# A second Strassen level in the first layer of a fused retention and MLP kernel

## The chip, the cores and the metric

The kernel runs on one core of a Trainium2 chip. The metric is the device time of one execution in microseconds (us), the median of the runs. A profile is one execution; its span runs from the first to the last instruction and is a little shorter than the device time.

Names used below: **TensorE** (PE in the profile) does matrix products, with PEld for the loading of its stationary operand; **VectorE** (DVE) and **ScalarE** (ACT) do elementwise work; GpSimd is POOL, and SyncE (SP) starts most of the DMAs. PSUM is the memory that TensorE writes into[...].

## The reference, cut to what matters

```python
def _attn_ref(q, k, v):                      # (4, 8, 768, 64) each: batch, heads, seq, head_dim
    gamma = 1.0 - 2.0 ** (-5.0 - np.arange(H, dtype=np.float32))
    for t in range(S):                       # retention: a state that decays, per head
        state = gamma * state + k[t] (outer) v[t]
        y[t] = scale * q[t] @ state

def _moe_ref(x, w_in, w_out):                # x (3072, 512), w_in (512, 2048), w_out (2048, 512)
    h = x @ w_in
    g = np.maximum(0.01 * h, h)              # leaky ReLU
    return (g @ w_out).astype(np.float32)
# reference: y becomes x, (batch*seq, heads*head_dim); the weights come in as float64
```

The two big products are the two layers, `x @ w_in` and `g @ w_out`. All of it is computed in fp32.

## The kernel before

The sequence is cut into six chunks of 128 time steps (times 4 batches: 512 tokens), and the 2048 hidden features into four units of 512. For each chunk `c` and unit `u` there is a first-layer step `hidden(c, u)` and a second-layer step `output`. Both are a 2x2 block product done by Strassen's scheme (in Winograd's form): seven products M1 to M7 of 256 x 256 x 256 blocks in place of eight, with sums of blocks made beforehand (`differences`, `add_sums`) and sums of products made afterwards (`takes`).

```python
def seven(tiles, name, takes, takes_piece=None, order=ORDER):
    banks = {}
    which = [("M1", "A", 0, 0), ("M6", "B", 5, 5), ("M5", "C", 4, 4), ("M4", "D", 3, 6),
             ("M2", "A", 2, 2), ("M7", "B", 1, 1), ("M3", "C", 6, 3)]
    for m, bank, sa, sb in (which[i] for i in order):
        ...                                       # a bank is [128, 2, 256] fp32: one PSUM bank
            for to, (i, a, z) in places:          # i = 0, 1: halves of the 256 output features
                for n, (w, x, t) in enumerate(tiles):
                    for k in range(2):
                        nc.tensor.matmul(to, lhsT=block(w, sa)[:, k, ts(i, 128)],
                                         rhs=rhs[:, k, a:z], start=..., stop=...)   # L585
            takes(m, ps)
        yield

def hidden(c, u, x, t, g, gd, order=ORDER):
    def leaky(i):
        nc.scalar.activation(g[:, i], g[:, i], AF.Prelu, alpha=0.01)                # L620
    def takes(m, ps):
        if m == "M1":
            nc.scalar.copy(out=got["m1"], in_=ps)                                   # L625
        elif m == "M6":
            plus(got["u2"], got["m1"], ps)                                          # L527
        elif m == "M5":
            nc.scalar.copy(out=got["m5"], in_=ps)
        elif m == "M4":
            got["m4"] = ps
        elif m == "M2":
            nc.scalar.activation(g[:, 0], ps, AF.Prelu, alpha=0.01)
        elif m == "M7":
            u3 = got["m1"]
            plus(u3, u3, ps)
            plus(g[:, 3], u3, got["m5"]);  leaky(3)
            plus(g[:, 2], u3, got["m4"]);  leaky(2)
        elif m == "M3":
            plus(g[:, 1], got["u2"], ps);  leaky(1)
            differences(g, gd)                                                      # L530
```

`output` has the same form, with nine VectorE additions where it adds to an earlier unit's result. Chunks 0 and 1 run together, unit by unit, while VectorE and ScalarE turn the float64 weights into fp32 (`round_piece`). From chunk 2 on, two units are done one after the other and their second layers are accumulated together in PSUM:

```python
for c in range(2, NC):
    for p in range(NU // 2):
        pair = []
        for u in (2 * p, 2 * p + 1):
            pair.append(new_g(c, u))
            run(hidden(c, u, *xs[c], *pair[-1][1:]), {})
        ...
        run(output(c, os[c], pair, p == 0, last), at)
        ...                        # visit_with_scores: the retention of the next chunk
```

## Time and profile before

| | before |
|---|---|
| device time, median of 2 runs | 657.12 us (656.94 to 657.3) |
| span of the profile | 655.4 us |
| PE busy | 650.6 us, 99% |
| DVE busy | 361.5 us, 55% |
| ACT busy | 176.1 us, 27% |
| DMA | 49.00 MB, mean 75 GB/s |
| DVE busy from 60 to 205 us (chunks 0 and 1) | 125.3 of 145 us |
| DVE busy from 344 us to the end | 124.3 of 311.4 us |

A row of the timeline gives the start of a run of like instructions, its length, the engine, the line, the operation, what it writes and reads, the tile's shape and how many there are; "[2.65 <-DVE g L527]" is the idle time of the engine before it and what ended it. An fp32 matmul appears as two records of TensorE, so "x8" is four matmuls. Records overlap[...]: the pace is read from the starts, not from the lengths.

### The profile page before, as it was taken

The page shows a single profiled execution, that of the slowest core. Times are in us where ns is not written, and L with a number is a line of the kernel's source. Part 1 is how long each engine was busy: PE and PEld are TensorE (multiplying, and loading weights), DVE is VectorE, ACT ScalarE, POOL GpSimd, SP SyncE. Part 2 cuts the span into 40 slices and gives each one's busy share as a digit, 9 for nine tenths or more (in the row PEclk, how much of TensorE's full clock was granted, in tenths as well). Part 3 has the DMA queues.
Part 4 walks back from the last instruction along what each step waited for, and adds up shares of the span by engine and source line. Part 5 has one row for each costly group of instructions (what it writes and reads, how often), then busy time and mean ns, then how long its engine had stood idle before and what let it go on. Part 6 is the DMA issues. An engine that isn't in the chain of part 4 may idle for free.

```text
span 655.4 us, 11361 instructions
## 1 busy us (share of the span) xinstructions
PE 650.6 (99%) x4937; PEld 568.2 (87%) x4937; DVE 361.5 (55%) x590; ACT 176.1 (27%) x323; POOL 22.7 (3%) x45
## 2 busy tenths in 40 slices
PE   8999999999999999999999999999999999999998
PEld 5888888888888888888888889888888888888887
DVE  5789969889887664243436414527423344431342
ACT  5855464264261003102102211300220210221210
POOL 1000000000000020000001001001000100000000
DMA  9921312323322650030022003005001001000001
GB/s 337 406 98 37 125 64 97 97 66 111 115 78 82 243 179 0 1 129 2 1 103 91 1 1 130 1 17 179 0 1 61 5 1 49 17 0 1 1 0 65
DMA packets 15906, 49.00 MB, mean 75 GB/s; under 512 B 1768, under 2 KB 2152, under 8 KB 15856
## 3 DMA queue, kind: packets, MB, share of 16 engines
q1 hardware_dynamic: 15696, 47.72, 20.7%
q8 instruction: 39, 0.64, 0.4%
q10 hardware_dynamic: 160, 0.55, 0.2%
q14 instruction: 11, 0.09, 0.0%
HBM read 41.97 MB, written 6.29 MB: 74 GB/s over the span
## 4 chain that ended last, share of the span: by engine, by line
PE 98%; DMA 1%; DVE 0%; ACT 0%; SPq 0%; issue 0%
PE B_o L585 13%; PE A_o L585 13%; PE C_o L585 13%; PE A_h L585 12%; PE B_h L585 12%; PE C_h L585 12%; PE D_o L585 6%; PE D_h L585 6%; PE ap L182 2%; PE d L607 2%; PE yp L255 2%; PE yp L219 1%; DMA raw<-in_weights_dram 1%; PE yp L244 1%; PE sp L270 1%; PE yp L270 0%
## 5 line engine op out<-in xcount | busy, mean ns | idle before, releaser
L585 PE MATMUL A_h<-x,w 128*128 128x256 f32 x368 | 87.7, 381 | 0.0
L585 PEld LDWEIGHTS A_h<-x,w 128*128 128x128 f32 x368 | 69.3, 190 | 9.6
L585 PE MATMUL A_o<-g,w 128*128 128x256 f32 x288 | 68.1, 379 | 0.0
L527 DVE TENSOR_TENSOR m<-m,B_h 128x512 f32<-128x512 f32 x23 | 15.8, 686 | 93.3 <-PE B_h L585 93.3
L585 PEld LDWEIGHTS A_o<-g,w 128*128 128x128 f32 x288 | 54.6, 190 | 7.5
L620 ACT ACTIVATE g<-g 128x512 f32<-128x512 f32 x69 | 42.0, 630 | 66.3 <-DVE g L527 66.3
L625 ACT COPY m<-A_h 128x512 f32<-128x512 f32 x23 | 13.5, 585 | 169.3 <-PE A_h L585 149.0
L527 DVE TENSOR_TENSOR m<-m,B_o 128x512 f32<-128x512 f32 x16 | 11.0, 685 | 64.4 <-PE B_o L585 64.4
L585 PE MATMUL B_h<-t,w 128*128 128x256 f32 x184 | 43.7, 380 | 0.0
L585 PE MATMUL C_h<-x,w 128*128 128x256 f32 x184 | 43.5, 379 | 0.0
L585 PE MATMUL C_h<-t,w 128*128 128x256 f32 x184 | 43.5, 379 | 0.0
L585 PE MATMUL D_h<-t,w 128*128 128x256 f32 x184 | 43.5, 379 | 0.0
L585 PE MATMUL B_h<-x,w 128*128 128x256 f32 x184 | 43.5, 379 | 0.0
L585 PEld LDWEIGHTS B_h<-t,w 128*128 128x128 f32 x184 | 34.7, 190 | 5.2 <-DVE t L530 0.6
L585 PEld LDWEIGHTS C_h<-x,w 128*128 128x128 f32 x184 | 35.0, 190 | 4.8
L585 PEld LDWEIGHTS D_h<-t,w 128*128 128x128 f32 x184 | 35.0, 190 | 4.8
L585 PEld LDWEIGHTS C_h<-t,w 128*128 128x128 f32 x184 | 35.0, 190 | 4.8
L585 PEld LDWEIGHTS B_h<-x,w 128*128 128x128 f32 x184 | 35.0, 190 | 4.8
L585 PE MATMUL C_o<-gd,w 128*128 128x256 f32 (+1 forms) x148 | 34.2, 373 | 0.0
L585 PE MATMUL C_o<-g,w 128*128 128x256 f32 (+1 forms) x148 | 34.2, 373 | 0.0
L530 DVE TENSOR_TENSOR gd<-g,gd 128x512 f32<-128x512 f32 x48 | 33.2, 692 | 1.7
L585 PE MATMUL B_o<-gd,w 128*128 128x256 f32 x144 | 34.1, 380 | 0.0
(131 smaller groups left out, 984.6 us busy)
## 6 DMA issues: line engine op xcount, KB each, us to landing
raw<-in_weights_dram SPq DMA_DIRECT2D x31, 512.0 KB, 3.9
kv<-in_kv_dram SPq DMA_DIRECT2D x17, 512.0 KB, 5.0
out_dram<-o SPq DMA_DIRECT2D x23, 256.0 KB, 2.1
qk<-in_qk_dram SPq DMA_DIRECT2D x10, 512.0 KB, 4.6
o<-in_qk_dram SPq DMA_DIRECT2D x8, 512.0 KB, 4.9
in<-in_qk_dram SPq DMA_DIRECT2D x5, 512.0 KB, 8.4
in<-in_kv_dram SPq DMA_DIRECT2D x3, 512.0 KB, 7.9
kv<-in_kv_dram SPq DMA_DIRECT2D x4, 256.0 KB, 7.4
```

Source lines behind the costliest of these rows:

```text
L182: nc.tensor.matmul(to, lhsT=x[ts(j, 64), 1, a, ts(late, 64)], rhs=x[ts(j, 64), 0, a, late * 64 :])
L219: mm = nc.tensor.matmul(ps[ts(i, 64), j, m, :], lhsT=st[b][ts(j, 64), a, :], rhs=x[ts(j, 64), 0, a, :], start=(m == 0), stop=False, skip_g ...
L244: mm = nc.tensor.matmul(ps[ts(i, 64), j, m, 0:64], lhsT=y[ts(s, 64), 1, 2 * a + j, :], rhs=am[ts(s, 64), j, m, 0], start=False, stop=True, ...
L255: nc.tensor.matmul(ps[ts(i, 64), j, m, 64:], lhsT=y[:, 1, 2 * a + j, :], rhs=am[:, j, m, 1 + (i ^ j)], start=(c == 0 and m == 0), stop=Tru ...
L270: nc.tensor.matmul(sp[ts(j, 64), a, :], lhsT=y[:, 0, 2 * a + j, :], rhs=y[:, 1, 2 * a + j, :], start=start, stop=True, skip_group_check=True)
L527: nc.vector.tensor_tensor(out=out, in0=a, in1=b, op=ALU.add)
L530: nc.vector.tensor_tensor(out=out, in0=a, in1=b, op=ALU.subtract)
L585: nc.tensor.matmul(to, lhsT=block(w, sa)[:, k, ts(i, 128)], rhs=rhs[:, k, a:z], start=(first and (i == 0 or split) and n == 0 and k == 0), ...
L607: nc.tensor.matmul(banks[r][:, i, :], lhsT=block(2 * u, r + 2 * kh)[:, k, ts(i, 128)], rhs=x[:, 2 * kh + th, k, :], start=(step == 0 and i ...
L620: nc.scalar.activation(g[:, i], g[:, i], AF.Prelu, alpha=0.01)
L625: nc.scalar.copy(out=got["m1"], in_=ps)
```

## The change

The first layer of chunks 2 to 5 gets a second Strassen level. Each of the seven 256 x 256 x 256 products M1 to M7 becomes seven products of 128 x 128 x 128: 49 matmuls of 128 moving columns in place of 28 of 256 columns. The aim is fewer columns on TensorE. The sums of weights that the inner level needs are made once by VectorE while chunks 0 and 1 run, stored in DRAM (`kept`), and loaded again for each chunk and unit. The outer products are done in two groups, of four and of three, so that one inner product for all of a group fits one PSUM bank.

A second idea runs through the whole kernel: instead of VectorE adding M1 and M6, ScalarE copies M1 into the PSUM bank in which M6 is then accumulated. TensorE then adds M6 (and M7) to it. [...]a small bf16 matmul (`fill`) goes through it. The order of the seven products changes with this.

```diff
+    kept = [dram.tile([128, 7, 7, C], FP32, name=f"kept_{u}") for u in range(NU)]
+        def do():                          # sum_of_unit: 4 of these for each of 4 units
+            if i == 0:   plus(s[0], a21, a22)          # each [128, 7, 128]
+            elif i == 1: minus(s[1], s[0], a11)
 ...
-    ORDER = (0, 1, 2, 3, 4, 5, 6)
+    ORDER = (0, 2, 1, 3, 4, 6, 5)
+    FUSED = (0, 2, 1, 4, 5, 6, 3)          # M1, M5, M6, M2, M7, M3, M4
+    LAST = (0, 2, 1, 3, 4, 5, 6)
 ...  hidden, now for chunks 0 and 1 alone
             if m == "M1":
-                got["m1"] = temp("m1", at)
-                nc.scalar.copy(out=got["m1"], in_=ps)
+                nc.scalar.copy(out=to, in_=ps)         # to = bank_of("B")
             elif m == "M6":
-                plus(got["u2"], got["m1"], ps)
+                nc.scalar.copy(out=got["u2"], in_=ps)
 ...  output
+            elif m == "M7":
+                if fused:
+                    nc.scalar.copy(out=bank_of("D"), in_=ps)   # M4 accumulates on it
+                add(3, ps)
 ...  the first layer of chunks 2 to 5
+    INNER = (("M1", 0, 0, 0), ("M5", 1, 3, 2), ("M4", 2, 2, 4), ("M6", 3, 4, 3), ("M2", 0, 1, 1),
+             ("M3", 1, 5, 5), ("M7", 3, 6, 6))
+    def inner(n, group):
+        w, count = ((wa, 4), (wb, 3))[group]
+        for m, q, j, s in INNER:
+            for i in range(count):
+                nc.tensor.matmul(ps[q][:, i], lhsT=w[:, j, i], rhs=part_of(moving[i], s),
+                                 start=(i == 0 and m in ("M1", "M5", "M4")), stop=True, ...)
+            if m == "M1":   nc.scalar.copy(out=ps[3], in_=ps[0])
+            elif m == "M5": nc.scalar.copy(out=sums[:, 3], in_=ps[1])
+            elif m == "M4": nc.scalar.copy(out=sums[:, 2], in_=ps[2])
+            elif m == "M6": nc.scalar.copy(out=sums[:, 1], in_=ps[3])
+            elif m == "M2": nc.scalar.copy(out=sums[:, 0], in_=ps[0])
+            elif m == "M3": plus(sums[:, 1], sums[:, 1], ps[1])
+            elif m == "M7":
+                plus(sums[:, 3], sums[:, 3], ps[3])
+                plus(sums[:, 2], sums[:, 2], ps[3])
+        load_unit(n + 1, group)             # the next unit's weights, by DMA
+
+    def outer(n, group):
+        if group == 0:
+            plus(u2, u2, m1)
+            plus(to(1), u2, m5)
+            return
+        plus(to(0), m1, m2);    leaky(0)    # leaky: ScalarE, to(i): a block of g
+        plus(to(1), to(1), m3); leaky(1)
+        plus(u2, u2, m7)
+        plus(to(3), u2, m5);    leaky(3)
+        plus(to(2), u2, m4);    leaky(2)
 ...
+    for n in range(N2):                     # 16: chunk 2 + n // 4, unit n % 4
+        if n + 1 < N2:
+            differences(*gs[n][1:])
+            inner(n + 1, 0)
+            outer(n + 1, 0)
+        if visiting:                        # retention of the next chunk, at units 0 and 1
+            joint_visit(...)
+        steps = output(c, os[c], [gs.pop(n)], ..., order=FUSED if more else LAST)
+        products(steps, 4)                  # M1, M5, M6, M2
+        if visiting:
+            fill(3)
+        ...
+        if more:
+            inner(n + 1, 1)
+            outer(n + 1, 1)
+        products(steps, 3)                  # M7, M3, M4
```

The second layers of two units are no longer accumulated together; each unit has an `output` of its own. The retention of the chunks 3 to 5 (`joint_visit`) uses the same matmuls as before in banks 4 to 7.

## The prediction

> **What bounds the kernel now.** I read the page's busy line first, then the chain of work that ended last, then the timeline of a quiet stretch, and last the windows by stage.

> ```profile
> PE 650.6 (99%) x4937; PEld 568.2 (87%) x4937; DVE 361.5 (55%) x590; ACT 176.1 (27%) x323; POOL 22.7 (3%) x45
> PE 98%; DMA 1%; DVE 0%; ACT 0%; SPq 0%; issue 0%
> ```

> TensorE is busy throughout and is 98% of the chain: any column taken off it is time saved, and any wait put on it is time lost. Its busy time alone could hide gaps, so I look at starts. From 406 to 414 us of the timeline, first-layer products and what follows them:

> ```profile
> 406.11 1.89 PE L585 MATMUL B_h<-x,w 128*128 128x256 f32 x8
> 407.83 1.89 PE L585 MATMUL C_h<-x,w 128*128 128x256 f32 x8
> 408.03 0.69 DVE L527 TENSOR_TENSOR m<-m,B_h 128x512 f32<-128x512 f32 x1 [6.15 <-PE B_h L585]
> 408.82 0.69 DVE L527 TENSOR_TENSOR g<-m,m 128x512 f32<-128x512 f32 x1
> 409.43 0.68 DVE L527 TENSOR_TENSOR g<-m,D_h 128x512 f32<-128x512 f32 x1
> 409.55 1.83 ACT L620 ACTIVATE g<-g 128x512 f32<-128x512 f32 x3 [2.65 <-DVE g L527]
> 409.56 1.89 PE L585 MATMUL A_h<-x,w 128*128 128x256 f32 x8
> 411.49 0.58 ACT L625 COPY m<-A_h 128x512 f32<-128x512 f32 x1
> ```

> Four matmuls start every 1.727 us, without a gap. A step of seven is 12.09 us. The reader should also see the chain after M7: VectorE starts 0.20 us after TensorE has gone on; a following addition starts 0.79 us later if it needs the last result and 0.61 us later if not; ScalarE's leaky ReLU starts 0.04 us after its input; the copy behind the three leaky ReLUs starts only when they end.

> The kernel has a few matmuls of 128 columns already, at its very end:

> ```profile
> 645.48 1.03 PE L585 MATMUL B_o<-g,w 128*128 128x256 f32 x4
> 646.34 1.03 PE L585 MATMUL B_o<-g,last 128*128 128x256 f32 x4
> ...
> 651.10 0.61 PE L585 MATMUL C_o<-g,last_s 128*128 128x128 f32 x4
> 651.55 0.61 PE L585 MATMUL C_o<-g,w 128*128 128x128 f32 x4
> 652.00 0.61 PE L585 MATMUL C_o<-g,last_s 128*128 128x128 f32 x4
> ```

> Two matmuls of 256 columns start every 0.865 us, two of 128 every 0.45 us: 0.432 and 0.225 us each.

> [...]half the columns cost 52% of the time (0.225 of 0.432 us), although each record here loads new weights.[...] No copy into PSUM is in the trace before.[...] The reloaded weights come in runs of 512, 1024 and 1536 B. The trace before has mostly runs of 3 KB and tells nothing of these.

> **The change, part by part.**

> TensorE, first layer of chunks 2 to 5: 28 x 0.432 = 12.10 us becomes 49 x 0.225 = 11.03 us. Sixteen times 1.07 is **-17.1 us**. The second layer keeps its columns, and so does retention.

> VectorE: an addition of 512 elements is 0.69 us, one of 384 is 0.553 us (the masking row of that shape). Per unit, the inner level has 3 x 0.69 + 3 x 0.553 = 3.7 us, the outer sums 7 x 0.69 = 4.8, the differences of g 4 x 0.69 = 2.8, the second layer 6 x 0.69 = 4.1: 15.4 us, with retention and the sums of x about 79 us a chunk, beside 11.03 + 12.10 us of TensorE a unit and 5 us for each of two visits, 102 us a chunk. So VectorE goes from 40% in this stretch (124.3 of 311.4 us) to over 75%, but isn't the bound on average. The question is its latency where TensorE needs it.

> I go through the order of one iteration of the new loop, with E the moment when TensorE has issued the last matmul of inner group 1. On TensorE follow M7, M3 and M4 of the second layer, 1.73 us each. M4 accumulates on bank D, into which ScalarE must first copy M7. In ScalarE's queue this copy stands behind the four leaky ReLUs of the unit just made, and they wait for VectorE's outer sums:

> - E + 0.20: VectorE adds the inner M7 to two sums of 384 elements, the second 0.47 us later (0.61 us, less 128 elements at about 1 ns, which is the slope between the two shapes).
> - the block g0 needs that: E + 1.25. Then g1 and u2 at 0.61 us each, g3 after u2 (0.72 to 0.79 us), g2 0.61 us later: it starts at E + 3.8 and ends at E + 4.5.
> - its leaky ReLU: E + 4.5 to E + 5.15. The copy of M7, 0.585 us: E + 5.7. With a hop to TensorE: **E + 5.8**.
> - TensorE without a wait would start M4 at E + 3.45.

> So TensorE waits **2.35 us** before M4, in each of the 15 iterations that have a next unit. Nothing gives it back, since TensorE is the bound. **+35 us.**

> Other waits I looked at and take as nothing: M6 of the second layer waits for the copy of M1, but M5's 1.73 us lie between; the inner M6 waits for the copy of the inner M1, with 1.35 us (M5 and M4 of the three) against about 0.8; the differences of g end at about E + 11, the next second layer begins at E + 13.8.

> Entering the new loop: the first inner group follows the first unit's leaky ReLUs closely, and its M6 waits for a copy in the same queue: +1.5 us. Thirteen fill matmuls, some 0.25 us each: +3 us. In the last visits no scores hide the taking of tokens: +0.7 us.

> Chunks 0 and 1: VectorE is 86% busy there (125.3 of 145 us). Each step of seven loses two additions (some 15 steps, -20 us of VectorE), the weight sums add sixteen of 896 elements, 1.08 us each by the same slope (+17 us). It stays as full as before, and where three tasks meet, around unit 3's retention, TensorE may wait a little: +3 us, a guess.

> DMA: a unit's weights are 49 blocks of 64 KB, 3.2 MB, in about 25.5 us: 126 GB/s, below the 406 GB/s that a slice of the page shows. The larger group (1.84 MB) has some 19 us from its release to its use. I take it as hidden.

> Sum: 657.1 - 17.1 + 35 + 1.5 + 3 + 0.7 + 3 = 683; I say **682 us**.

> **The rivals.**

> - *The copy does not hold M4 up*, because the chain is shorter than I built it. Then about 648 us remain, 1.4% faster. For it: the intent of the change, and an average load of VectorE of 75%. Against: the queue order, which I take as fixed, and seven additions in a row of which none is under 0.47 us.
> - *The 128-column matmuls run slower in the mass*[...]. Then there is no gain in columns: with 0.25 us instead of 0.225, 16 x 49 x 0.025 = 20 us more, so near 700. For it: only sixteen records of that shape are in the trace. Against: those are evenly spaced.
> - *The reload of weights comes late*[...]: the inner groups would start with a wait on DMA, at 100 GB/s about as long as the window. Then over 690 us. Against: the windows of nearly 20 us and few other transfers.
> - *VectorE becomes the bound in chunks 0 and 1*: at most the 14% free there turns negative; I'd expect up to 10 us.

> **Range and chances.** The wait can be 1.5 to 3 us (22 to 45 us in all), the rest 2 to 12 us against the sure -17: 665 to 695 us. To be slower by over 2% (above 670.3) the wait has to be over some 1.5 us; to be faster by over 2% (below 644) all of my extra terms would have to vanish and more. Hence 0.04 faster, 0.22 same, 0.74 slower.

> **What would show it.** In the profile after, the inner matmuls should start every 0.225 us, or 6.3 and 4.7 us a group. The waits should have TensorE waiting for the M7 copy, about 2.3 us, 15 times, seen as a gap before the product into bank 6, with four leaky ReLUs and then a copy into bank 6 on ScalarE just ahead. VectorE should be near 75% busy there. I am wrong if that gap is under 1 us, if gaps before the inner groups end on DMA, or if the first part (up to the start of the new loop, 237 us before) has moved by more than 8 us.

## The result, and the profile after

The changed kernel takes **718.38 us** (718.01 to 718.76, two runs): 1.0933 times the kernel before [1.0901, 1.0965]. It is 61.3 us slower, where the prediction had 682 us and a range up to 695. The direction and the main wait were foreseen; the size was not.

The page of the kernel after: the busy line, the clock granted to TensorE in 40 slices, and the chain that ended last.

```profile
PE 665.6 (93%) x5583; PEld 590.7 (82%) x5583; DVE 473.0 (66%) x782; ACT 265.1 (37%) x495; POOL 23.2 (3%) x45
...
PEclk9999999999999899999999999999999999999998
...
PE 78%; DVE 14%; ACT 4%; DMA 2%; issue 2%; DVEq 0%
```

TensorE was 99% busy and is 93% busy, and VectorE and ScalarE have entered the chain with 14% and 4%. There is a puzzle in the first line. The second level takes columns off TensorE, yet its busy time *rose* by 15 us, from 650.6 to 665.6. The clock line hides the reason: nearly every slice shows 9, which is "90% or more". The mean over the whole span is 0.963, against 1.000 before. A mean of 0.963 can be 3.7% everywhere or one half for a few us at a time.

The waits of TensorE in the kernel after (what waited and for what: us in total, times, longest):

```profile
PE bank L536 <- ACT bank L646: 32.0, 15, 2.1
PE bank L569 <- DVE o L480: 6.3, 1, 6.3
PE bank L156 <- issue: 3.2, 2, 2.7
...
PE bank L1036 <- DMA wa<-kept: 0.9, 1, 0.9
```

L646 is the copy of M7 into bank D, L536 the second-layer products (M4 here), L1036 the inner products, L569 a fill matmul, L156 the retention's scores. The predicted wait is there, 15 times. The timeline shows what follows it. One iteration on TensorE, starts and lengths in us:

```profile
556.15 3.62 PE L536 MATMUL bank<-g,w 128*128 128x256 f32 x16
561.91 3.66 PE L536 MATMUL bank<-gd,w 128*128 128x256 f32 x8 [2.13 <-ACT bank L646]
565.40 0.39 PE L1036 MATMUL bank<-x,wa 128*128 128x128 f32 x2
...
578.57 4.85 PE L1036 MATMUL bank<-x,wb 128*128 128x128 f32 x42
583.25 3.62 PE L536 MATMUL bank<-g,w 128*128 128x256 f32 x16
589.01 3.62 PE L536 MATMUL bank<-gd,w 128*128 128x256 f32 x8 [2.13 <-ACT bank L646]
```

The first row is M7 and M3, sixteen records in 3.62 us. The row after it is M4, eight records of the same shape in 3.66 us: half the pace. From M4's start to the next product is 3.49 us where M4 took 1.73. In windows of 1 us around that wait (window, its length, PE busy and number of records, granted clock, DMA share, GB/s):

```profile
560.00:561.00 1.00, 0.00 (x0) 1.00 1.12 349
561.00:562.00 1.00, 0.09 (x1) 0.95 1.18 285
562.00:563.00 1.00, 1.00 (x3) 0.50 0.16 37
563.00:564.00 1.00, 1.00 (x4) 0.50 0.00 0
...
565.00:566.00 1.00, 1.00 (x8) 0.84 0.00 0
566.00:567.00 1.00, 1.00 (x12) 1.00 0.00 0
```

The clock is one half right behind the wait, for about 3.4 us, and then whole again. TensorE counts as busy all the while, which is why its busy time rose. The prediction has no such term.

To count these, I took windows of 8.2 us, from the moment TensorE stops, around each of the 15 waits. In twelve the mean clock is about 0.79. In three (waits that end at 382.93, 502.37 and 532.61 us) it stays at 1.00. One of each kind, same columns:

```profile
353.65:361.85 8.20, 6.07 (x32) 0.79 0.34 101
380.73:388.93 8.20, 6.07 (x47) 1.00 0.60 191
```

The wait is equally long in both; 32 records pass in one and 47 in the other. So a wait costs 2.13 us, and in twelve cases 8.2 x 0.21 = 1.72 us more. That is 20.6 us in all, over half as much again as the waits themselves.

On ScalarE the wait ends as the prediction drew it:

```profile
585.30 1.23 ACT L1070 ACTIVATE g<-g 128x512 f32<-128x512 f32 x2 [2.71 <-DVE g L480]
587.24 1.23 ACT L1070 ACTIVATE g<-g 128x512 f32<-128x512 f32 x2 [0.70 <-DVE g L480]
588.37 0.58 ACT L646 COPY bank<-bank 128x512 f32<-128x512 f32 x1
```

Four leaky ReLUs (L1070), each released by VectorE, then the copy, and M4 at 589.01.

**An account of the +61.3 us**, from the trace after:

| | us | from |
|---|---|---|
| fewer columns, 16 units | -18 | 12.09 - 10.95 each |
| M4 waits for the copy, 15 times | +32.0 | waits |
| halved clock after twelve of these | +20.6 | 1.72 each |
| the first part, up to the end of the new loop's first unit (both inner groups) | +13 | 261.1 us, against 237.0 + 10.95 |
| standstills in the visits (2.74, 0.44, 0.75) and the clock after one | +5.6 | "issue" in the waits and timeline |
| fills in the visits | +2 | ten of 0.16 to 0.22 |
| one wait on reloaded weights | +0.9 | waits |
| not assigned | +5 | remainder |

The first part is measured up to the same work in both traces: in the one before to the first product of chunk 2 (first row), in the one after to the first product of its second unit (second row), which lies one first-layer unit, 10.95 us, further on:

```profile
237.01 1.99 PE L585 MATMUL A_h<-x,w 128*128 128x256 f32 x8
...
261.08 0.38 PE L1036 MATMUL bank<-x,wa 128*128 128x128 f32 x2
```

Of its 13 us, 6.3 are one wait and some 1.9 the halved clock behind it. The timeline at that place:

```profile
230.95 1.15 DVE L483 TENSOR_TENSOR x<-t,x 128x384 f32<-128x384 f32 x2
...
232.48 1.28 DVE L480 TENSOR_TENSOR o<-o,B_o 128x512 f32<-128x512 f32 x2
...
233.82 1.03 PE L569 MATMUL bank<-mask 128*128 128x512 bf16 x2 [6.34 <-DVE o L480]
```

Here TensorE's banks pass from the old loop to the new one. The additions of the last old step (`o<-o,B_o`) stand in VectorE's queue behind the sums of chunk 2's x, and the first fill of the new loop waits for them.

### The profile page after: what moved, and what is told of

It reads as the page before. It is cut to its first block, busy times and chain, and to the rows that moved or that the text cites. A ratio compares the mean times of both kernels' runs of the same rounds, so it can differ in the third digit from the quotient of the medians.

```text
span 717.0 us, 13274 instructions
## 1 busy us (share of the span) xinstructions
PE 665.6 (93%) x5583; PEld 590.7 (82%) x5583; DVE 473.0 (66%) x782; ACT 265.1 (37%) x495; POOL 23.2 (3%) x45
## 4 chain that ended last, share of the span: by engine, by line
PE 78%; DVE 14%; ACT 4%; DMA 2%; issue 2%; DVEq 0%
PE bank L1036 25%; PE bank L536 24%; DVE g L480 4%; DVE made L480 3%; PE A_o L536 3%; PE C_h L536 3%; PE B_h L536 3%; ACT g L1070 3%; PE B_o L536 2%; PE A_h L536 2%; PE C_o L536 2%; PE d L557 2%; PE D_o L536 2%; PE D_h L536 1%; DMA wa<-kept 1%
## 5 line engine op out<-in xcount | busy, mean ns | idle before, releaser
L480 DVE TENSOR_TENSOR o<-o,bank 128x512 f32<-128x512 f32 (+2 forms) x91 | 58.7, 662 | 83.6 <-PE bank L536 65.3
L536 PE MATMUL bank<-gd,w 128*128 128x256 f32 x288 | 79.2, 431 | 26.3 <-ACT bank L646 25.6
L536 PEld LDWEIGHTS bank<-gd,w 128*128 128x128 f32 x288 | 59.7, 211 | 40.6 <-ACT bank L646 30.4
L536 PE MATMUL bank<-g,w 128*128 128x256 f32 x384 | 91.0, 386 | 0.3 <-DVE x L269 0.3
L536 PEld LDWEIGHTS bank<-g,w 128*128 128x128 f32 x384 | 72.2, 193 | 10.2 <-DVE x L269 0.5
L1036 PEld LDWEIGHTS bank<-x,wb 128*128 128x128 f32 x672 | 77.6, 192 | 1.4
L1036 PE MATMUL bank<-x,wb 128*128 128x128 f32 x672 | 77.6, 275 | 0.0
L1036 PE MATMUL bank<-x,wa 128*128 128x128 f32 x512 | 71.0, 282 | 0.0
L1036 PEld LDWEIGHTS bank<-x,wa 128*128 128x128 f32 x512 | 67.8, 201 | 2.5 <-ACT bank L1040 0.2
L1070 ACT ACTIVATE g<-g 128x512 f32<-128x512 f32 x64 | 39.4, 630 | 54.6 <-DVE g L480 54.6
L1036 PE MATMUL bank<-t,wa 128*128 128x128 f32 x384 | 57.4, 289 | 0.9 <-DMA wa<-kept 0.9
L1036 PEld LDWEIGHTS bank<-t,wa 128*128 128x128 f32 x384 | 52.5, 207 | 1.1 <-DMA wa<-kept 1.1
L536 PE MATMUL bank<-gd,last 128*128 128x256 f32 (+1 forms) x124 | 29.1, 389 | 6.4 <-ACT bank L646 6.4
L536 PEld LDWEIGHTS bank<-gd,last 128*128 128x128 f32 x124 | 23.4, 197 | 10.8 <-ACT bank L646 7.6
L536 PE MATMUL bank<-g,last 128*128 128x256 f32 x120 | 30.5, 403 | 0.0
L536 PEld LDWEIGHTS bank<-g,last 128*128 128x128 f32 x120 | 24.2, 206 | 3.9 <-issue 0.3
L536 PE MATMUL A_h<-x,w 128*128 128x256 f32 x112 | 26.6, 380 | 0.0
```

The lines of the kernel that those rows point to most:

```text
L480: nc.vector.tensor_tensor(out=out, in0=a, in1=b, op=ALU.add)
L536: nc.tensor.matmul(to, lhsT=block(w, sa)[:, k, ts(i, 128)], rhs=rhs[:, k, a:z], start=(first and (i == 0 or split) and n == 0 and k == 0), ...
L1036: nc.tensor.matmul(ps[q][:, i], lhsT=w[:, j, i], rhs=part_of(moving[i], s), start=(i == 0 and m in ("M1", "M5", "M4")), stop=True, skip_gr ...
```

## The experiments

Each kernel is timed against the kernel before on the same chip (657.4 to 657.5 us there). The first four start from the kernel after.

**The copy of M7 ahead of the leaky ReLUs.** M7 is computed right after the inner group, so its copy enters ScalarE's queue before the four leaky ReLUs.

```diff
             inner(n + 1, 1)
+            products(steps, 1)
             outer(n + 1, 1)
...
-        products(steps, 3)
+        products(steps, 2 if more else 3)
```

> Theory A: in the changed kernel TensorE waits 2.13 us before M4 in 15 iterations because the copy of M7 into M4's bank stands behind four leaky ReLUs in ScalarE's queue, and in 12 of these a halved TensorE clock follows for about 3.4 us and costs 1.7 us more. Here the second layer's M7, its copy and its addition are issued ahead of the outer sums; the work is the same. A expects no gap before M4, no halved clock in the loop, 15 x 2.13 + 12 x 1.72 = 52.6 us less than 718.4, so 666 us. Rival B, that the clock falls because the matmuls are short and dense and not because of the gap: only the 32 us of waiting go, 686 us, and the clock stays at about 0.96. Rival C, that the wait comes back elsewhere because VectorE's outer sums now begin later: a new wait on VectorE before the next second layer, 675 us or more.

Measured: 666.81 us, ratio 1.0142 [1.011, 1.0174], mean clock 0.992. No wait on the copy is left. Fifty-two us come from the order of one copy in a queue; that is 32.0 + 20.6 to within about 1 us. So the place in the queue holds M4, not the copy's own time, and the clock's loss hangs on that wait.

**Filler: is it the idle time that halves the clock?** Here the wait stays, but TensorE works through it: ten (or five) bf16 fill matmuls into a bank that is free.

```diff
-        products(steps, 3)
+        products(steps, 2)
+        for _ in range(10 if more else 0):     # 5 in the second kernel
+            fill(0)
+        products(steps, 1)
```

> The changed kernel with ten bf16 matmuls of 512 columns, about 2.15 us in all, put into the gap before M4, into a bank that nobody reads. They do not remove the wait, they only keep TensorE at work during it. Theory A (an idle stretch of 2.1 us brings on the halved clock): the clock stays at 1.0 in the loop, M4 starts as late as before, 718.4 - 12 x 1.72 = 698 us. Rival B (the clock follows the density of the matmuls): no change or worse, 718 to 722 us.

> As with ten, but five such matmuls, 1.08 us, so that 1.05 us of the gap stays idle. If the clock needs a longer idle stretch than about 1 us to fall, 698 us as with ten; if any idle stretch brings it on, 718 us. I have no strong view, 60 to 40 for the first.

Measured: 694.84 us with ten, ratio 1.0569 [1.0548, 1.059], and 703.82 us with five, 1.0706 [1.0672, 1.0739]. TensorE's timeline with ten:

```profile
546.00 2.32 PE L569 MATMUL bank<-mask 128*128 128x512 bf16 x10
548.29 1.99 PE L536 MATMUL bank<-gd,w 128*128 128x256 f32 x8
550.12 0.38 PE L1036 MATMUL bank<-x,wa 128*128 128x128 f32 x2
```

M4 is held by 2.29 us, no less than before, but now runs at full pace (1.83 us to the next product). An iteration takes 25.43 us (546.00 to 571.43) in place of 27.1. Work that computes nothing made the kernel 23.5 us faster, so here the halved clock comes from TensorE standing idle, not from the burst of matmuls behind the wait. (It is 3 us more than the 20.6 because the standstills in the visits were shorter as well, 1.2 us against 3.9, with no halved clock behind them.)

With five, an idle wait remains:

```profile
PE bank L536 <- ACT bank L646: 15.8, 15, 1.1
```

None of the fifteen is followed by a drop, and its iterations take 25.43 us too. Yet the kernel is 9 us slower than with ten, so its expectation of 698 was missed. The difference lies outside the iterations' M4: standstills of 5.8 us against 1.2, a wait of 1.9 us on weights against 0.6, and halved clock after each of the longer ones.

**M7 added by VectorE.** The other way to take the wait out: no copy into bank D, one more addition on VectorE, and M4 ahead of M2.

```diff
-                       order=FUSED if more else LAST)
+                       order=LAST)
```

> The changed kernel with the second layer of chunks 2 to 5 in the order M1, M5, M6, M4 and then, after inner group 1, M2, M7, M3, and with VectorE adding M7 to the third block, in place of ScalarE's copy of M7 into M4's bank. So no product of the last three waits for ScalarE. VectorE has one addition of 0.69 us more per unit. Theory A: no gap, 666 us, the same as with the copy moved ahead. If instead the fuller VectorE is what holds TensorE: 670 us or more, with waits on VectorE.

Measured: 664.74 us, ratio 1.012 [1.0099, 1.0141], clock 0.995. Fifteen additions on VectorE cost TensorE nothing. Beginning this sum in PSUM by a copy bought nothing at this place.

**The entry mended**, on top of the last. The sums of chunk 2's x move behind the last old step's additions, half of them after the scores.

```diff
-                     s3=[next_heads], s4=[differ(2)], s5=[sums(2, 0)], s6=[sums(2, 1)]),
+                     s3=[next_heads], s6=[differ(2), sums(2, 0)]),
...
+    sums_of_x(2, 1)
     products(last, 2)
```

> The kernel with the sum by VectorE, and at the entry of the new loop the differences and inner sums of chunk 2's x moved behind the last additions of chunk 0's second layer, so that VectorE gives PSUM's banks back sooner. Theory: the 6.5 us for which TensorE waits for VectorE's additions to o at the handover of PSUM, and the halved clock after it, come from VectorE's queue order. Then that wait falls to 1 to 2 us, the clock stays up there, and the kernel takes 664.7 - 5 - 1.7 = 658 us, level with the kernel before (657.5). Rival: the handover of the PSUM pools itself costs this time; then the wait stays at over 5 us and the time at 664 us.

Measured: 658.75 us, ratio 1.0014 [1.0006, 1.0022]. The wait of the fill fell from 6.5 to 1.4 us. The order in VectorE's queue was the cause; handing the banks over is not by itself dear.

Now the two kernels are level, though the second level saves 18 us. The first part is still 6.9 us longer (it ends at 254.83 us, against 237.0 + 10.95). The other large item is standstills with no releaser, "issue" in the waits: 3.1, 0.9 and 2.1 us, two of them with a halved clock behind. They differ from one execution to the next: thirteen took 657.01 to 661.44 us, the profiled one being the longest, and the two with a mean clock of 1.000 took 657.01 and 657.34. The standstills occur in the visits, where many small matmuls run:

```profile
PE bank L156 <- issue: 3.9, 2, 3.1
PE bank L536 <- issue: 2.1, 1, 2.1
```

The longest, in windows of 2 us:

```profile
294.00:296.00 2.00, 2.00 (x95) 1.00 1.03 360
296.00:298.00 2.00, 0.05 (x2) 1.00 1.06 383
298.00:300.00 2.00, 0.87 (x11) 1.00 1.04 412
300.00:302.00 2.00, 2.00 (x7) 0.51 1.02 408
```

First 95 short records in 2 us; then nothing, while the DMA engines are full at 360 to 412 GB/s; then the halved clock. My two theories: TensorE's own stream of instructions comes late because the DMA engines are full (L), or the visit has too many small matmuls in a row whatever the DMA does (D).

**The loads later in the program's order.** The next unit's weights and the next visit's inputs are issued after M1 of the second layer.

```diff
-        load_unit(n + 1, group)
+        if group == 1 or not hold[0]:
+            load_unit(n + 1, group)
...
+        products(steps, 1)
+        if visiting:
+            load_unit(n + 2, 0)
+            visit_loads(c + 1, 2 * u, later)
+        products(steps, 3)
```

> As the one before, and in the iterations with retention the loads of the next unit's weights (group 0) and of the next q, k and v are issued after the second layer's first product instead of before and during retention. In the traces so far TensorE stands still for 2.4 to 3.6 us in the scores of one visit with no releaser shown, while DMA moves 370 to 410 GB/s, and a halved clock follows. Theory: TensorE's instructions come late there because the loads fill the DMA engines. Then these stretches shrink below 1 us and 3 to 5 us go: 653 us, 0.6% faster than the kernel before. Rival: the standstill is bound to the place in the instruction stream and not to the loads: no change against the one before, or slower by a wait for the weights, whose window falls from about 19 to about 12 us.

Measured: 658.12 us, ratio 1.0008 [0.9998, 1.0017]. It tells nothing of the theories, because the edit did not do what I meant. The load of `wa` started no later than in the kernel it comes from (first row, here; second row, there):

```profile
290.92 0.52 SPq L1005 DMA_DIRECT2D wa<-kept  x1
...
290.52 0.52 SPq L1002 DMA_DIRECT2D wa<-kept  x1
```

Its place in the program did not hold it back, since nothing in that order made SyncE wait for TensorE. The standstill stayed, 2.8 us.

**The scores apart.** One of the two score steps of a visit, with what follows it (loads for later visits among that), moves behind M1 of the second layer, so the row of small matmuls is shorter. (The scores stand in banks 0 to 3.) It starts from the entry kernel.

```diff
-            score_apart(*at, banks=bank[2 * i : 2 * i + 2])     # both, in joint_visit
+        products(steps, 1)
+        if visiting:
+            second_score(c + 1, 2 * u, later)                   # one of them
+        products(steps, 3)
```

> As the kernel with the mended entry (658.75 us), but of the two score steps in each visit the second stands after the second layer's M1, so that 3.5 us of slower-issued matmuls of 256 columns lie between the two dense stretches of small ones. Theory D: TensorE outruns the arrival of its own instructions at the end of a long dense stretch. Then the standstill of 3.1 us in the second scores shrinks below 1.5 us and the halved clock after it goes: 655 us. Rival L, that the loads alone are at fault: the standstill moves but stays about as long, 658 to 660 us.

Measured: 655.73 us, ratio 0.9973 [0.9964, 0.9983], clock 0.999. The standstills in the visits shrank from 6.1 to 2.1 us (longest 1.1), and no halved clock followed. That is as D says, but the shorter row does not exclude L.

**The loads held.** As two kernels ago, with a real dependency: the first load waits for the last matmul of M1.

```diff
+            load = nc.sync.dma_start(out=wa[:, :, 0:1], in_=kept[u][:, :, 0:1])
+            if after is not None:                    # after: the last matmul of M1
+                tc.add_manual_dep(load.ins, after.ins.name, IN_ORDER, reason="after M1")
```

> The version with later loads again, this time with the loads truly held: in the version before they left as early as ever, since their place in the order is no wait. Here the first of them waits for the last matmul of the second layer's M1, so that the DMA engines are idle during the dense stretch of the visit. Theory L: the standstill of 2.8 us with no releaser, and the halved clock after it, go: 654 us. Theory D, that the dense stretch outruns the instructions whatever the loads do: the standstill stays at 2 us or more, 658 us. If the weights now come late: a wait on wa of some us, 660 us or more.

Measured: **651.78 us** (651.38 to 652.49, five runs), ratio 0.9914 [0.99, 0.9927], clock 1.000. The same four windows:

```profile
294.00:296.00 2.00, 2.00 (x89) 1.00 0.03 8
296.00:298.00 2.00, 2.00 (x68) 1.00 0.03 8
298.00:300.00 2.00, 2.00 (x11) 1.00 0.00 0
300.00:302.00 2.00, 2.00 (x11) 1.00 0.55 147
```

The row of small matmuls is as dense as ever, the DMA engines are idle, and TensorE does not stop. D alone falls. That the dense row is needed as well was not tested by itself: the kernel before this one shortened the row, but moved loads with it.

The views give these standstills no releaser. The page lists a DMA queue of the kind "instruction" (q8): 39 packets and 0.64 MB in the kernel before, 44 and 0.72 MB in the kernel after. In the trace of the kernel after, the three standstills in the visits (2.74, 0.44 and 0.75 us) end 1.44, 1.59 and 1.54 us after a packet of this queue has landed. The longest is from 306.35 to 309.09 us, beside DMA at 391 GB/s; its packet ran from 306.54 to 307.64 us, when TensorE had already stopped. That agrees with L, but it shows neither whose instructions the packet held nor how long it had waited before it ran. That TensorE lacked its instructions there, because the loads held them up, is my reading of it and was not shown.

This kernel is 0.9% faster than the one before the change. TensorE is 98% busy in it. An iteration of its loop on TensorE:

```profile
593.62 1.89 PE L541 MATMUL bank<-g,w 128*128 128x256 f32 x8
...
600.53 4.85 PE L1045 MATMUL bank<-x,wb 128*128 128x128 f32 x42
...
616.65 1.89 PE L541 MATMUL bank<-g,w 128*128 128x256 f32 x8
```

From 593.62 to 616.65 is 23.03 us, which is 12.09 for the second layer and 10.94 for the first: no wait is left in it. Of the 18 us, 5.7 reach the time. The rest goes to the first part (it ends at 255.39 us, against 237.0 + 10.95, 7.4 us), a wait of 1.6 us on `wa` in the second unit, fills, and small gaps. That wait does not come from holding the loads, for this load is not held; the other kernels with the second level have 0.2 to 1.9 us at this place. I did not take these apart further.

## Why the prediction was wrong in size, point by point

- **Columns: right.** Predicted 0.225 us a matmul and -17.1 us; 42 records (21 matmuls) in 583.25 - 578.57 = 4.68 us are 0.223 each, a unit 10.95 us, -18 us. The rival of slow 128-column matmuls falls.
- **The wait before M4: right.** Predicted 2.35 us, 15 times, 35 us; measured 2.13, 15 times, 32.0, by the queue order that was drawn. The rival that the copy would not hold M4 falls, and the experiment that moved the copy shows its cause. One reading behind it was no evidence: the copy at 411.49 us, taken as a sign that ScalarE keeps its order, copies a product whose matmuls ran from 409.56 to 411.45 us, so it could not have started earlier in any order. The trace after does show the order: M7's matmuls start at 583.25 us and take 1.73, and its copy starts only at 588.37, behind the leaky ReLUs.
- **What a wait costs: the step that failed.** "Nothing gives it back" was right, but the sum took a wait of 2.35 us to cost 2.35 us. Twelve of the fifteen were followed by a half clock worth 1.72 us each. The filler kernel isolates it. This term of 20.6 us was absent from the prediction; it is more than half of the 36 us between 682 and the result.
- **Entering the new loop: mis-sized.** Predicted +1.5 for a copy, and +3 in chunks 0 and 1, "a guess". Measured +13 for the first part. The guess for chunks 0 and 1 was fair: their last first-layer step starts at 191.11 us, at 188.54 before. The other 10 us came at the entry. The prediction named a shift over 8 us there as a sign of being wrong, and I had the wrong queue: it was VectorE's, as the entry kernel shows.
- **Fills and tokens: right.** About 0.22 us a fill against "some 0.25", and 0.3 us for the tokens against 0.7.
- **The reload of weights: hidden, as a transfer.** One wait of 0.9 us. But the full DMA beside a visit went with a standstill of 2.74 us and its clock loss, which the prediction did not consider.
- **VectorE near 75%: not in this kernel.** It is 60% busy in the loop, 214.57 of 360 us, since the loop is slower. In the last kernel it is 206.44 of 296 us, 70%. It was never the bound.
- **The range** rested on the length of the wait, which came out as said, so it was too narrow for a cost that had not been thought of. The mean clock of the kernel before was 1.000, and TensorE hardly stood idle in its loop: a trace without waits cannot tell what a wait costs.

## What to carry to other kernels

When a change puts a wait on a TensorE that had none, look at the granted clock just behind the wait in windows of 1 us: here twelve of fifteen waits of 2.13 us cost 3.85 us each, and ten matmuls that compute nothing told the idle time from other causes in one run. When ScalarE or VectorE hands something to TensorE, place that instruction in its queue before the work that TensorE does not need yet; the place of one copy was worth some 52 us here. And moving a load in the program did not delay it (290.92 us, against 290.52 without the move), while a dependency did (8 GB/s where there had been 360 and 383): if a load must not run beside something, give it one.
